# Linear attention and a two-layer FFN on one core: the fourth group's first product as seven half-size products

## The chip, the cores and the metric

The kernel runs on one core of one Trainium2 chip. The metric is the device time of one execution in microseconds (us); less is better. The core has five engines with instruction streams of their own: PE (TensorE, matrix products, with its weight loads shown as PEld), DVE (VectorE), ACT (ScalarE), POOL (GpSimd) and SP (SyncE, which here only issues DMAs). Each engine works through its own instructions in the order in which they were written, and waits at each for what it needs from the others.

## What is computed

The reference, cut to its core (B, H, S, D = 8, 8, 576, 64; the FFN's widths are 512 and 2048):

```
r = lambda x, w: np.maximum(x, 0) * w
q_p = concat(r(q, cos), r(q, sin));  k_p = concat(r(k, cos), r(k, sin))   # 128 features
kv  = einsum('bhsf,bhsd->bhfd', k_p, v);   z = sum(k_p over s)
x   = einsum('bhsf,bhfd->bhsd', q_p, kv) / (einsum('bhsf,bhf->bhs', q_p, z) + 1e-6)
h   = x @ w_in                      # (4608, 512) @ (512, 2048)
out = maximum(0.01 * h, h) @ w_out  # (4608, 2048) @ (2048, 512)
```

cos and sin depend on the position in the sequence alone.

## The kernel before

The 4608 tokens are worked in nine groups of 512 tokens: groups 0 to 7 are the first 512 tokens of batches 0 to 7, and group 8 gathers the last 64 tokens of every batch. "The fourth group" is group 3. For each batch and group these steps follow each other:

- loads of q, k and v (SP, L121 and L135), each into a staging buffer; k of batches 1 and 3 lies in the buffer `wext`.
- k's feature map, `k_token` (L253 on DVE and POOL, L251 on ACT): 9 pieces with cosine and 9 with sine, "kp" below; there is **one** kp buffer, so the pieces of batch b+1 can be written only when the kv sum of batch b is done. `v_pairs` casts v into the buffer vm (also one).
- `kv_sum` (L326): 72 small matmuls in a row, the "kv sum"; ACT copies the result out (L333).
- `q_prep`: q's feature map, four pieces of two instructions (cosine, sine), in two buffers of two pieces ("pairs"); each pair is transposed by a DMA (L363).
- `num` (L400): four times eight small matmuls, and DVE's division (L411, L415, L416) into xs; a DMA transposes xs into xT (L377).
- the first product of the FFN, x times w_in, with the leaky ReLU that gives g.
- the second product, g times w_out, and the stores of the output.

The two FFN products are done in two ways. The plain way (`ffn1`, L474): 16 units of four matmuls of 512 columns, every second one followed by one activation of 1024 columns on ACT (L482). The other way splits both factors in halves and multiplies seven times instead of eight (Winograd's form of Strassen's algorithm): seven half-size products and a number of sums. In the second product (`ffn2s`, L733) this is used from group 1 on. The sums of the weights are made once (`weight_sum`), the sums of g by DVE for each group (`g_sum`, all L526).

In the first product (`ffn1s`, L626) it is used from group F7 = 4 on. A group has four parts u; in each, seven products of four matmuls of 256 columns, and on the way seven evictions of 512 columns on ACT and two sums on DVE (`ffn1e`): b, s and u copy PSUM (L640, L642, L644), y and z add (DVE, L526), a, c, e and d are the leaky ReLU (L652). A part uses three of four PSUM banks, which rotate. It needs the sums W of w_in, made once (`w1_sum`: numbers 1, 2 and 4 go into `wext`, number 3 is made in place in w_in and so waits for the last plain first product), and four sums X of xT for each group (`x_sum`).

What sets the order is written out by hand in two layers. PE's work after the beginning is a list of *units*, each with a position: group g's second product and group g+1's first product share the positions 16g to 16g+16. All other work is a list of *steps*, each with a position out of the table TUNE; `weave` issues, ahead of every unit, the steps whose position has been reached. TUNE gives for each batch b: "kc", "ks" the places of the 18 kp pieces, "q", "v", "n" (num), "mm" (kv sum), "qT" and "x" (transposes), "L" (loads), and "e", a string that says which engine does what: four letters for q, nine for kc, nine for ks, two for v (P POOL, D DVE, A ACT). "S", "S4s", "W", "X", "T" place the sums, "We" and "Xe" their engines. Where the first product is split, the string "O" gives the order of a part: digits are products, F is half a unit of the second product, letters are evictions. "ahead" tells how many units of the second product stand before the first product of the next group begins (for groups 1 and 2).

Of the kernel before, what the change touches and what calls it, by code (L numbers as in the profile page):

```python
# [16 lines left out]
T = 9  # L17
# [3 lines left out]
def kernel(  # L21
# [15 lines left out]
    B, H, S, D = q.shape  # L37
# [12 lines left out]
    NG = B + 1  # L50
    NE = D + 2
    G7 = 1
    F7 = 4

    ctx.enter_context(tc.manual_schedule())

# [31 lines left out]
    def need(*keys):  # L88
        for key in keys:
            assert key in done, key  # L90
# [154 lines left out]
    kv = [const.tile([P, H, NE], dt.float16, name=f"kv{b}") for b in range(B)]  # L245
# [319 lines left out]
        )  # L565

    def w1_sum(bp, n, eng):
        need(("kv", 3), *(("W", bp, i) for i in {1: (), 2: (1,), 4: (2,), 3: (1,)}[n]))
        if n == 3:
            need(("f1", F7 - 1))  # L570
        done.add(("W", bp, n))
        a11, a12, a21, a22 = (w1_quarter(bp, r, d) for r in range(2) for d in range(2))
        o1, o2, o4 = (SW[i][:, bp] for i in (1, 2, 4))
        if n == 1:
            tt_op(o1, a21, a22, ALU.add, eng)
        elif n == 2:
            tt_op(o2, o1, a11, ALU.subtract, eng)
        elif n == 3:
            tt_op(a21, a11, a21, ALU.subtract, eng)
        else:  # L580
            tt_op(o4, a12, o2, ALU.subtract, eng)

    def x_sum(g, n, eng):
        need(("xT", g), *(("X", g, i) for i in {1: (), 2: (1,), 4: (2,), 3: (1,)}[n]))
        if g > F7 and n in (2, 4):
            need(("f1", g - 1))
# [213 lines left out]
    held = []  # L800
# [24 lines left out]
    for hg in range(2):  # L825
        for j in range(J):
            e = ACT if j == 3 else POOL if hg == 1 and j == 2 else DVE
# [81 lines left out]
    def f2h(g, i):  # L909
        return lambda: ffn2s(g, i // 2, (i % 2,))  # L910
# [37 lines left out]
    order = [(tt, part) for part in range(3) for tt in range(J)]  # L948
# [45 lines left out]
    for m in range(6, NFT):  # L994
        units.append((8 + m / 2, f1(1, m)))

    TUNE = {'B': {2: {'L': None,
               'e': 'PDPDDDPPDADDDPPDAAAADADD',
               'kc': [9.77, 8.81, 11.63, 10.39, 5.8, 11.57, 6.05, 9.36, 10.09],
               'ks': [9.53, 8.49, 7.12, 10.33, 12.5, 12.31, 11.64, 10.89, 9.62],  # L1000
               'mm': 13.64,
               'n': [14.2, 15.14, 16.53, 17.13],
               'q': [8.35, 8.73, 8.87, 10.0],
               'qT': [10.83, 11.12],
               'v': [8.01, 10.09],
               'x': 17.37},
           3: {'L': [2.08, 11.11, 12.82, 15.77],
               'e': 'AAAPAPADDADPAAAAAADAPADS',
               'kc': [20.89, 22.22, 20.65, 20.01, 23.27, 23.44, 20.62, 21.9, 18.49],
               'ks': [15.15, 17.93, 17.14, 16.06, 17.76, 21.94, 20.89, 19.82, 24.95],  # L1010
               'mm': 26.16,
               'n': [26.78, 28.23, 28.78, 29.48],
               'q': [15.64, 18.8, 13.77, 18.62],
               'qT': [18.98, 19.88],
               'v': [21.71, 21.6],
               'x': 30.73},
           4: {'L': [16.71, 21.32, 20.14, 20.14],
               'e': 'PADDDAADAADDAAAADDDDDDDP',
               'kc': [30.62, 29.57, 31.25, 31.74, 33.43, 33.08, 32.79, 33.57, 35.66],
               'ks': [32.92, 32.9, 30.68, 36.1, 37.07, 36.25, 36.42, 34.07, 32.95],  # L1020
               'mm': 38.04,
               'n': [39.1, 41.29, 42.88, 43.81],
               'q': [32.62, 34.78, 35.82, 36.19],
               'qT': [35.22, 37.11],
               'v': [32.65, 35.2],
               'x': 44.12},
           5: {'L': [34.11, 29.18, 40.16, 40.16],
               'e': 'ADADAAAPAAADPDADAAAPDDAP',
               'kc': [38.44, 38.15, 38.92, 39.32, 40.87, 41.72, 40.0, 43.78, 40.87],
               'ks': [38.93, 38.71, 39.75, 41.84, 41.1, 38.82, 43.11, 39.83, 43.81],  # L1030
               'mm': 47.03,
               'n': [47.67, 52.31, 51.34, 53.28],
               'q': [39.37, 39.97, 39.48, 43.05],
               'qT': [43.05, 44.13],
               'v': [43.91, 42.87],
               'x': 54.54},
           6: {'L': [42.28, 44.22, 45.5, 45.5],
               'e': 'ADAAPPPPDPDPADPADPDPAPPP',
               'kc': [53.18, 53.74, 53.6, 52.91, 53.27, 55.16, 55.42, 56.13, 58.02],
               'ks': [52.77, 51.75, 53.37, 52.12, 55.91, 60.22, 57.04, 53.88, 59.03],  # L1040
               'mm': 61.88,
               'n': [65.52, 67.68, 69.17, 71.27],
               'q': [53.1, 56.98, 57.05, 58.94],
               'qT': [58.17, 60.13],
               'v': [58.06, 56.62],
               'x': 71.75},
           7: {'L': [56.13, 58.67, 61.31, 61.31],
               'e': 'ADADDPAPADDDAAPPDAAAADPP',
               'kc': [66.43, 65.11, 67.46, 69.35, 71.81, 72.94, 73.77, 75.44, 76.57],
               'ks': [66.11, 68.9, 68.79, 69.21, 69.83, 69.79, 72.94, 73.3, 73.64],  # L1050
               'mm': 77.65,
               'n': [79.76, 83.09, 85.27, 87.09],
               'q': [68.45, 70.19, 73.41, 73.73],
               'qT': [74.58, 77.29],
               'v': [70.0, 75.7],
               'x': 91.06},
           8: {'L': [80.3, 80.97, 83.67, 84.3],
               'e': 'PDAD',
               'kc': [],
               'ks': [],  # L1060
               'mm': 1.77,
               'n': [96.19, 98.15, 99.61, 101.69],
               'q': [86.42, 87.09, 90.14, 91.17],
               'qT': [90.6, 94.58],
               'v': [],
               'x': 103.69}},
     'O': ['1b5sFF6uFF2a7yF3zcFFe4d', '1b5sFF6uF2a7yF3zcFe4dFF'],
     'S': {1: [12.21, 12.8, 18.14, 13.88, 15.3, 17.98],
           2: [26.26, 26.46, 33.47, 28.81, 29.6, 33.81],
           3: [44.93, 46.66, 45.74, 46.54, 46.47, 48.84],  # L1070
           4: [60.19, 61.22, 64.88, 60.45, 61.59, 65.79, 65.07],
           5: [75.6, 76.13, 80.5, 77.09, 78.7, 83.16, 81.99],
           6: [91.23, 91.98, 96.48, 92.12, 94.25, 96.16, 97.15],
           7: [107.64, 109.18, 113.66, 109.45, 110.7, 111.07, 111.38],
           8: [123.3, 125.17, 130.52, 123.94, 125.59, 128.31, 129.84]},
     'S4': 25.16,
     'S4s': {2: [41.14, 41.26],
             3: [56.09, 55.22],
             4: [71.56, 71.4],
             5: [88.97, 89.77],  # L1080
             6: [104.5, 104.51],
             7: [119.89, 120.83]},
     'T': [8.99, 12.77, 9.59, 14.6],
     'W': [[31.24, 32.96, 34.8, 47.53], [37.35, 38.58, 38.89, 48.2]],
     'We': ['PPDD', 'PDDP'],
     'X': {4: [47.03, 47.24, 49.45, 47.13],
           5: [61.4, 63.54, 63.57, 62.66],
           6: [77.84, 79.15, 79.25, 78.62],
           7: [94.22, 95.69, 96.01, 95.7],
           8: [109.08, 112.39, 113.4, 111.16]},  # L1090
     'Xe': {4: 'DPPD', 5: 'PDPD', 6: 'PPPP', 7: 'DDPP', 8: 'PPDD'},
     'ahead': [12, 7],
     'held': 9.31}

    for g in range(1, NG):
        last = 14
        ahead = {1: TUNE["ahead"][0], 2: TUNE["ahead"][1], NG - 1: last}.get(g, 0)
        order = [f2(g, i) for i in range(ahead)]
        left = last - ahead
        if F7 <= g + 1 < NG:  # L1100
            n = i = 0
            for u in range(4):
                for c in TUNE["O"][u == 3]:
                    if c == "F":
                        order.append((n, f2h(g, 2 * ahead + i)))
                        i += 1
                    elif c.isdigit():
                        order.append((n, f1p(g + 1, u, int(c))))
                    else:
                        order.append((n - 1 + E_AT[c], f1e(g + 1, u, c)))  # L1110
                    n += c == "F" or c.isdigit()
            assert i == 28, i
            units += [(16 * g + 16 * p / n, u) for p, u in order]
            continue
        elif g + 1 < NG:
            behind = [-(-16 * (k + 1) // left) - 1 for k in range(left)]
            for i in range(16):
                order.append(f1(g + 1, i))
                order += [f2(g, ahead + k) for k in range(left) if behind[k] == i]
        for n, u in enumerate(order):  # L1120
            units.append((16 * g + 16 * n / len(order), u))
# [30 lines left out]
    for b, t in TUNE["B"].items():  # L1152
        e = [engines[c] for c in t["e"]]
# [57 lines left out]
```

## Time and profile before

| | us |
|---|---|
| median of 3 runs | 276.87 |
| the runs | 278.65, 276.87, 276.69 |
| profiled execution, its own time | 276.07 |
| of it, span from the first to the last instruction | 274.3 |
| DVE, ACT, POOL busy in the span | 196.2, 180.4, 101.1 |

Positions and times go together as follows: position 16 (group 1's second product) begins 68.7 us after the span's start, position 32 at about 97.5, the kv sums of batches 2, 3, 4 and 5 stand at 61.3, 85.7, 107.9 and 125.1. In the rows of the profile, a line such as `L253 POOL TENSOR_SCALAR kp<-kst,cos_t 128x256 f16<-128x256 f32 x12 | 15.4, 1292 | 15.9 <-PE ...` gives line, engine, operation, output and inputs, sizes and count; then busy us and the mean ns of one; then the engine's idle time before them and what ended it. A row of a timeline gives start, length, and what; `x72` is 72 instructions in a row. L253 and L526 are lines of helpers, so the tile names tell what a row is: kp is k's map, qp q's, vm the cast v, wext and w the sums W, X and xT the sums X, g and ext the sums of g, y and ps_f the additions y and z.

### The profile page before, as it was taken

The page shows a single profiled execution, that of the slowest core. Times are in us where ns is not written, and L with a number is a line of the kernel's source. Part 1 is how long each engine was busy: PE and PEld are TensorE (multiplying, and loading weights), DVE is VectorE, ACT ScalarE, POOL GpSimd, SP SyncE. Part 2 cuts the span into 40 slices and gives each one's busy share as a digit, 9 for nine tenths or more (in the row PEclk, how much of TensorE's full clock was granted, in tenths as well). Part 3 has the DMA queues.
Part 4 walks back from the last instruction along what each step waited for, and adds up shares of the span by engine and source line. Part 5 has one row for each costly group of instructions (what it writes and reads, how often), then busy time and mean ns, then how long its engine had stood idle before and what let it go on. Part 6 is the DMA issues. An engine that isn't in the chain of part 4 may idle for free.

```text
span 274.3 us, 6865 instructions
## 1 busy us (share of the span) xinstructions
PE 265.5 (97%) x2813; PEld 212.0 (77%) x2813; DVE 196.2 (72%) x401; ACT 180.4 (66%) x310; POOL 101.1 (37%) x84
## 2 busy tenths in 40 slices
PE   7899999999999999999999999999999999999994
PEld 2575464655976586677999999999998899999983
DVE  4850597799863678786988789986798658646752
ACT  7857447497825556974898599866775567676500
POOL 2576002998509600323899290515003003000000
PEclk9999999999999999999999999999999999999999
DMA  7999999999999879999979974936475052111124
GB/s 240 358 395 410 382 400 372 376 227 291 301 179 299 322 176 238 260 229 176 377 160 256 263 235 104 196 89 146 103 165 126 4 117 76 41 38 41 60 58 115
DMA packets 77119, 57.59 MB, mean 210 GB/s; under 512 B 49312, under 2 KB 65696, under 8 KB 76704
## 3 DMA queue, kind: packets, MB, share of 16 engines
q1 hardware_dynamic: 76480, 56.63, 73.0%
q10 hardware_dynamic: 608, 0.52, 0.6%
q8 instruction: 22, 0.36, 0.6%
q14 instruction: 9, 0.07, 0.1%
HBM read 36.70 MB, written 9.44 MB: 168 GB/s over the span
## 4 chain that ended last, share of the span: by engine, by line
PE 71%; DMA 18%; POOL 4%; DVE 3%; SPq 2%; issue 2%; ACT 0%; POOLq 0%; DVEq 0%
PE ps L733 33%; PE ps_f L626 22%; DMA qst<-in_q_dram 10%; PE ps_h L474 10%; DMA wext<-in_moe_w_in_dram 4%; DMA qpT<-qp 3%; PE ps_num L400 3%; PE ps_kv L326 2%; POOL qp L253 2%; POOL kp L253 2%; PE ps_f L733 1%; SPq L135 1%; SPq L167 1%; DVE xs L416 1%; DVE ext L526 0%
## 5 line engine op out<-in xcount | busy, mean ns | idle before, releaser
L733 PEld LDWEIGHTS <-g 128*128 128x128 f16 x640 | 61.7, 98 | 8.2 <-ACT g L482 0.6
L733 PE MATMUL ps<-w,g 128*128 128x256 f16 x496 | 64.8, 273 | 0.4 <-ACT g L482 0.4
L474 PE MATMUL ps_h<-xT,w 128*128 128x512 f16 (+1 forms) x272 | 59.3, 367 | 0.1
L482 ACT ACTIVATE g<-ps_h 128x1024 f16<-128x1024 f32 x32 | 32.2, 1023 | 23.9 <-PE ps_h L474 23.9
L474 PEld LDWEIGHTS <-w 128*128 128x128 f16 x272 | 29.6, 114 | 20.6
L652 ACT ACTIVATE g<-ps_f 128x512 f16<-128x512 f32 x60 | 34.7, 596 | 8.5 <-PE ps_f L626 6.1
L626 PEld LDWEIGHTS <-w 128*128 128x128 f16 x320 | 34.6, 114 | 0.8
L626 PE MATMUL ps_f<-xT,w 128*128 128x256 f16 x240 | 33.3, 273 | 0.0
L733 PE MATMUL ps<-T,ext 128*128 128x256 f16 x240 | 32.1, 273 | 0.0
L733 PEld LDWEIGHTS <-ext 128*128 128x128 f16 x256 | 24.8, 98 | 3.1 <-issue 0.2
L626 PEld LDWEIGHTS <-wext 128*128 128x128 f16 x240 | 26.4, 113 | 0.8 <-issue 0.2
L253 POOL TENSOR_SCALAR kp<-kst,cos_t 128x256 f16<-128x256 f32 (+1 forms) x15 | 18.2, 1225 | 18.7 <-PE ps_kv L326 15.9
L526 DVE TENSOR_TENSOR ext<-g 128x512 f16<-128x512 f16 (+1 forms) x23 | 14.6, 640 | 12.1 <-ACT g L482 10.0
L526 DVE TENSOR_TENSOR y<-ps_f,s 128x512 f32<-128x512 f32 x20 | 13.8, 689 | 11.0 <-PE ps_f L626 9.1
L526 DVE TENSOR_TENSOR ext<-ps,ext 128x512 f32<-128x512 f32 x16 | 11.0, 690 | 12.8 <-PE ps L733 11.7
L416 DVE TENSOR_TENSOR xs<-ps_num,rden 128x512 f16<-128x512 f32 x28 | 19.4, 691 | 1.0
L626 PE MATMUL ps_f<-X,wext 128*128 128x256 f16 x128 | 19.2, 272 | 0.0
L652 ACT ACTIVATE g<-y 128x512 f16<-128x512 f32 x20 | 12.6, 630 | 9.2 <-DVE y L526 9.2
L644 ACT COPY u<-ps_f 128x512 f32<-128x512 f32 x20 | 11.7, 587 | 10.2 <-PE ps_f L626 10.1
L526 DVE TENSOR_TENSOR osb<-ps,ext 128x512 f32<-128x512 f32 x23 | 15.8, 685 | 3.7 <-PE ps L733 3.7
L526 POOL TENSOR_TENSOR X<-xT,X 128x512 f16<-128x512 f16 x7 | 8.8, 1262 | 22.9 <-PE ps_f L626 16.1
L733 PE MATMUL ps<-ext,g 128*128 128x256 f16 x128 | 17.1, 272 | 0.0
(116 smaller groups left out, 444.5 us busy)
## 6 DMA issues: line engine op xcount, KB each, us to landing
out_dram<-osb SPq DMA_DIRECT2D x32, 256.0 KB, 3.2
qst<-in_q_dram SPq DMA_DIRECT2D x7, 1024.0 KB, 8.0
kst<-in_k_dram SPq DMA_DIRECT2D x5, 1152.0 KB, 9.0
vst<-in_v_dram SPq DMA_DIRECT2D x5, 1152.0 KB, 7.5
w2st<-in_moe_w_out_dram SPq DMA_DIRECT2D x3, 1024.0 KB, 12.8
vst<-in_v_dram SPq DMA_DIRECT2D x4, 576.0 KB, 6.6
ext<-in_moe_w_in_dram SPq DMA_DIRECT2D x4, 512.0 KB, 10.7
kst<-in_k_dram SPq DMA_DIRECT2D x2, 576.0 KB, 7.5
```

The lines of the kernel that those rows point to most:

```text
L135: nc.sync.dma_start(st[nm, b][:, sl].rearrange("p c j d -> p c (j d)"), rows[:, sl])
L253: eng.tensor_scalar(out=o, in0=i, scalar1=0.0, scalar2=col, op0=ALU.max, op1=ALU.mult)
L326: nc.tensor.matmul(ps[:, o, (c - lo) * NE : (c - lo + 1) * NE], lhsT=st["kp", b][sl, c, j, :], rhs=vm[sl, c, j, :], start=(j == 0), stop=( ...
L400: nc.tensor.matmul(ps[lo:hi, h // 4, (h % 4) * NE : (h % 4 + 1) * NE], lhsT=qpT[:, h, lo:hi], rhs=kv[b][:, h, :],)
L416: nc.vector.tensor_tensor(out=xs, in0=ps[:, :, 0 : 4 * NE].rearrange("p a (b e) -> p a b e", e=NE)[:, :, :, 0:D], in1=rden.rearrange("p (a ...
L474: nc.tensor.matmul(ps[:, m % 2, lo:hi], lhsT=w1[m // 4, c][0][:, w1[m // 4, c][1], m % 4 : 512 : 4], rhs=xT[:, lo // P : hi // P, c, :], s ...
L482: nc.scalar.activation(st["g", g][:, m - 1 : m + 1, :], ps, AF.Lrelu)
L526: eng.tensor_tensor(out=o, in0=a, in1=b, op=op)
L626: nc.tensor.matmul(ps[:, mi * HT : (mi + 1) * HT], lhsT=a[:, c, 2 * r0 + mi : 512 : 4], rhs=b[:, c], start=(n in (1, 5) and mi == 0 and c ...
L644: nc.scalar.copy(u1, B_)
L652: nc.scalar.activation(st["g", g][:, m : m + 2, r * HT : (r + 1) * HT], {"a": A, "c": y22, "e": E, "d": B_}[e].rearrange("p (m t) -> p m t ...
L733: nc.tensor.matmul(ps[:, tt], lhsT=a[:, i, tt * P : (tt + 1) * P], rhs=b[:, i], start=(first and i == 0), stop=(i == NPR - 1 and (apart or ...
```

## The change

Group 3's first product is done as seven half-size products too (F7 = 3), so its 16 plain units and 8 activations leave, and 28 products with 28 evictions on ACT and 8 sums on DVE come. It needs four sums X for group 3. The W sums are placed earlier (their position moves from 31.24 to 24.80 for the first, from 48.2 to 35.67 for the last), and `w1_sum` asks for the kp pieces of batch 3 instead of its kv sum. In group 2's second product 8 units (16 halves) stand ahead instead of 7, and the 12 halves that are left lie in the parts of group 3's first product by four new strings of "O". The places and engines of most steps of batches 2 to 5 are set anew, those of 6 to 8 slightly.

```
-    F7 = 4
+    F7 = 3
...
     def w1_sum(bp, n, eng):
-        need(("kv", 3), *(("W", bp, i) for i in {1: (), 2: (1,), 4: (2,), 3: (1,)}[n]))
+        need(*(("kp", 3, j, f, 0) for j in range(T) for f in (0, D)), *(("W", bp, i) for i in {1: (), 2: (1,), 4: (2,), 3: (1,)}[n]))
...
     TUNE = {'B': {2: {'L': None,
-               'e': 'PDPDDDPPDADDDPPDAAAADADD',
+               'e': 'PDPDDDPPDADDPPPAPAAADDDD',
...
-               'q': [8.35, 8.73, 8.87, 10.0],
+               'q': [7.49, 7.91, 9.16, 10.33],
...
            3:
-               'e': 'AAAPAPADDADPAAAAAADAPADS',
+               'e': 'APAPPPAPDDAPAAAAAPAADAAA',
...
            4:
-               'e': 'PADDDAADAADDAAAADDDDDDDP',
+               'e': 'AADADAPAADPDAPDDDDPDDDDP',
...
            5:
-               'e': 'ADADAAAPAAADPDADAAAPDDAP',
+               'e': 'APAPPDPPPDPDDDDADPAPDDAP',
-               'kc': [38.44, 38.15, 38.92, 39.32, 40.87, 41.72, 40.0, 43.78, 40.87],
-               'ks': [38.93, 38.71, 39.75, 41.84, 41.1, 38.82, 43.11, 39.83, 43.81],
-               'mm': 47.03,
+               'kc': [39.02, 39.31, 41.53, 41.24, 40.23, 42.8, 42.37, 44.86, 42.56],
+               'ks': [40.41, 39.97, 41.78, 45.51, 44.13, 41.98, 45.77, 42.39, 46.09],
+               'mm': 47.0,
...
-     'O': ['1b5sFF6uFF2a7yF3zcFFe4d', '1b5sFF6uF2a7yF3zcFe4dFF'],
+     'O': ['1b5sF6u2aF7y3zcF4ed', '1b5sF6u2aF7y3zcF4ed', '1b5sF6u2aF7y3zcF4ed', '1b5sF6u2aF7y3zc4edF',
+           '1b5sFF6uFF2a7yF3zcFFe4d', '1b5sFF6uF2a7yF3zcFe4dFF'],
...
-     'W': [[31.24, 32.96, 34.8, 47.53], [37.35, 38.58, 38.89, 48.2]],
-     'We': ['PPDD', 'PDDP'],
-     'X': {4: [47.03, 47.24, 49.45, 47.13],
+     'W': [[24.8, 25.9, 27.1, 32.85], [29.07, 30.81, 32.09, 35.67]],
+     'We': ['PDPD', 'PPPD'],
+     'X': {3: [34.5, 35.23, 35.51, 37.21],
+           4: [46.97, 48.08, 49.48, 48.2],
...
-     'ahead': [12, 7],
-     'held': 9.31}
+     'ahead': [12, 8],
+     'held': 5.78}
...
         if F7 <= g + 1 < NG:
-            n = i = 0
+            order = [(i, f2h(g, i)) for i in range(2 * ahead)]
+            n = i = 2 * ahead
             for u in range(4):
-                for c in TUNE["O"][u == 3]:
+                for c in TUNE["O"][u if ahead else 4 + (u == 3)]:
                     if c == "F":
-                        order.append((n, f2h(g, 2 * ahead + i)))
+                        order.append((n, f2h(g, i)))
                         i += 1
```

POOL's order up to kv sum 2 was q, kp, q, kp, kp, kp (a q is one piece of two instructions) and becomes q, kp, kp, kp, q, kp, kp, kp. Between kv sums 4 and 5 POOL had kp, kp, v, kp and gets kp, q, kp, kp, kp, q, kp, v, kp, kp.

## The prediction

> **What bounds the kernel now.** I read the page first (busy time, slices), then the chain of waits, then the timelines of PE and POOL around the instructions that the change moves.
>
> ```profile
> span 274.3 us, 6865 instructions
> PE 265.5 (97%) x2813; PEld 212.0 (77%) x2813; DVE 196.2 (72%) x401; ACT 180.4 (66%) x310; POOL 101.1 (37%) x84
> ```
>
> PE is busy for 97% of the span, at a granted clock of 0.9 or more in all 40 slices. A matmul taken away is worth its whole pace, and every new wait of PE costs its whole length. The pace is read from the chain of waits:
>
> ```profile
> 107.93 1.25 PE ps_kv L326 x72
> ...
> 115.02 1.73 PE ps_h L474 x8
> 116.75 0.87 PE ps L733 x8
> ...
> 125.06 1.25 PE ps_kv L326 x72
> ```
>
> A 512-column matmul takes 1.73/8 = 0.216 us, a 256-column one 0.87/8 = 0.109 us. The two x72 rows are the kv sums of batches 4 and 5. Each reads all 18 kp pieces of its batch; there is one kp buffer, so no piece of batch 5 can be written before kv sum 4 has ended, and PE can't start kv sum 5 before the last piece is there. So the bracket from kv sum to kv sum (1) has a PE length and (2) must hold all kp work of one batch on each engine. Busy time by bracket (us; PE, PEld, DVE, ACT, POOL, each with its count):
>
> ```profile
> 86.91:107.93 21.02, 20.56 (x166) 14.08 (x166) 15.71 (x40) 11.31 (x18) 6.52 (x4) 1.00 0.88 265
> ...
> 109.18:125.06 15.88, 15.88 (x125) 10.25 (x126) 11.42 (x28) 12.87 (x21) 4.69 (x4) 1.00 0.94 240
> ...
> 126.31:150.16 23.85, 23.85 (x240) 21.94 (x242) 21.52 (x41) 19.41 (x36) 21.09 (x16) 1.00 0.99 246
> ```
>
> The second row is the bracket that the change fills most: POOL does only 4.69 us in 15.88. In the third POOL has 21.09 of 23.85 and PE still has no idle time.
>
> The third thing to see is that kv sum 2 has no slack today. POOL, then PE:
>
> ```profile
> 46.86 2.00 POOL L253 TENSOR_SCALAR qp<-qst,cos_t 128x512 f16<-128x512 f32 x1 [2.23 <-PE ps_o L500]
> 48.85 2.00 POOL L253 TENSOR_SCALAR qp<-qst,sin_t 128x512 f16<-128x512 f32 x1
> 50.82 1.14 POOL L253 TENSOR_SCALAR kp<-kst,sin_t 128x256 f16<-128x256 f32 x1
> 51.94 2.50 POOL L253 TENSOR_SCALAR qp<-qst,cos_t 128x512 f16<-128x512 f32 x1
> 54.42 2.15 POOL L253 TENSOR_SCALAR qp<-qst,sin_t 128x512 f16<-128x512 f32 x1
> 56.55 1.57 POOL L253 TENSOR_SCALAR kp<-kst,sin_t 128x256 f16<-128x256 f32 x1
> 58.11 3.24 POOL L253 TENSOR_SCALAR kp<-kst,cos_t 128x256 f16<-128x256 f32 x2
> ```
>
> ```profile
> 61.30 1.35 PE L326 MATMUL ps_kv<-vm,kp 64*128 64x66 f16 x72
> ...
> 68.07 0.28 PE L733 MATMUL ps<-w,g 128*128 128x256 f16 x1 [0.35 <-ACT g L482]
> 68.47 0.43 PE L400 MATMUL ps_num<-kv,qpT 128*128 128x66 f16 x8
> ```
>
> POOL's last kp piece ends at 58.11 + 3.24 = 61.35, and PE starts the sum at 61.30. Whatever is added to POOL before it, PE waits for.
>
> **The change part by part.** Prices on POOL come from the groups by shape:
>
> ```profile
> L253 POOL TENSOR_SCALAR kp<-kst,cos_t 128x256 f16<-128x256 f32 x12 | 15.4, 1292 | 15.9 <-PE ps_kv L326 15.9
> L253 POOL TENSOR_SCALAR kp<-kst,sin_t 128x256 f16<-128x256 f32 x9 | 11.9, 1328 | 1.1 <-DMA kst<-in_k_dram 1.1
> L253 POOL TENSOR_SCALAR qp<-qst,cos_t 128x512 f16<-128x512 f32 x4 | 9.0, 2255 | 2.2 <-PE ps_o L500 2.2
> L253 POOL TENSOR_SCALAR qp<-qst,sin_t 128x512 f16<-128x512 f32 x4 | 8.6, 2161 | 0.0
> L261 POOL CAST vm<-vst 128x1152 f16<-128x1152 f32 x6 | 7.0, 1176 | 4.3 <-DMA vst<-in_v_dram 4.3
> ```
>
> *PE's own work.* 16 units of 4 matmuls of 512 columns go (64 x 0.216 = 13.8), 28 products of 4 matmuls of 256 come (112 x 0.109 = 12.2): -1.6 us. The 28 halves of group 2's second product stay 28; one unit more of them stands ahead, which counts nothing. Weight loads: 112 for 64, but PEld has 21.94 of 23.85 in a bracket of such halves and PE is full there: nothing.
>
> *kv sum 2.* POOL's queue up to it was q, kp, q, kp x3; it becomes q, kp x3, q, kp x3: two pieces more. The first q waits for the same q load and starts at 46.86 as before. From 50.82: kp 1.14, two kp at about 1.36 (between 1.14 and 1.57), q 4.65, three kp at 1.6 (as 3.24/2), ends 64.1. PE waits 64.1 - 61.3 = 2.8. Ends: all at the fastest rows (1.14, 2.00) POOL is done at 46.86 + 8.0 + 6.8 = 61.7, +0.4; with all six at 1.6, +3.4. I take 2.8, since the neighbouring rows ran at that rate. What comes back: the q transpose of pair 1 (landing 68.42, PE at 68.47 after 0.29 idle) is issued about 1 us earlier and PE comes later, so that wait goes, and a 0.2 wait before the num at 65.66 (it waits for DVE's division) too: -0.5. The 0.35 for ACT's g stays; its cause is PE's own last unit. Net +2.3.
>
> *kv sum 2 to 4.* POOL gets four W sums (2.12 each) and the X sums 1 and 2 between kv sums 3 and 4, with 4 kp and a v: about 17.4 us where PE needs 19.3. What ends last there is xT of group 3, which landed at 99.58, 12.7 after kv sum 3's end: X1, X2 (1.26 each) and one kp behind it end at 16.5. Cover 2.8: costed at nothing. W sums that wait for each other across POOL and DVE hold DVE up for some 2.6 us where it idled 5.37 us before (86.76): nothing.
>
> *kv sum 4 to 5.* PE's nominal length: 31 products and halves x 0.437 = 13.55, four num x 0.26, together 14.6. POOL's queue in it: cos kp x5 (6.5), sin kp x2 (2.7), two q of two instructions (8.8), one v (1.2): 19.1 where it was 4.69. It starts 0.17 after kv sum 4 (109.35 against 109.18 before), and the piece that comes last is read 0.2 after the sum's start, so kv sum 5 starts at 19.1, not 14.6: +4.5. Ends: all at the fastest rows (1.14, 2.00, 1.15) 17.1, +2.5; all at rows slowed most (1.6, 2.5, 1.32) 22.5, +7.9. I take the means, because most of this batch's pieces lie beside DVE work of the mixed kind that made those means.
>
> *Evictions.* Eight L482 activations (1023 ns) become 28 of 0.59 us on ACT and eight additions of 0.69 on DVE. ACT has in this bracket 21 of them (12.4), two q (2.9), two kp (1.0), v 1.15 and kv 0.6: 18.0 by the row means, some 15.1 when starts overlap by the 0.1 us that the timeline shows: more than 14.6. Product 6 waits for copy b behind e and d, product 4 for y only one half (0.44) and product 3 after product 7. Following the order with these rows I find waits of PE of 0.1, 0.6, 0.4, 0.75, 0.25 and 0.5: 2.6 us, but they end before POOL's last piece: hidden under the 4.5. If POOL were in time, they would be what is left.
>
> *SP.* The q transposes of group 5 wait for POOL's q, and the loads of q, k, v 6 and x's transpose of group 4 stand behind them. Transpose 1 goes out about 14.2 after kv sum 4, k 6 at some 17 (17.9 before): no later against kv sum 5. Nothing.
>
> *Later groups.* Between kv sums 5 and 6 PE's length is 26.3 with 21.7 on POOL; between 6 and 7 22.4 with 8.8. ACT stays near 80%. PE's instructions cover this; at most 1 us if some step misses (the longest such wait before was 0.25, at 210.65).
>
> **Sum.** -1.6 + 2.3 + 4.5 = +5.2. On the profiled execution (276.07, of it 274.3 span) that is 281.3; its time lies 0.80 under the median of the runs (276.87), so the forecast for the median is 282.1.
>
> **A rule beside the rows.** POOL's kp took 1.14 at 135.69 (5.63 for five) while DVE mostly read PSUM, and 1.69 at 141.30 beside DVE's g<-g,ext with two inputs from SBUF. The Trainium skill, GPSIMD Engine Reference, section 1 "Specifications", says that POOL shares its SBUF interface with VectorE and contends with instructions of two SBUF inputs or of a 2-port mode; by that rule, the trace agrees, and the sum would come out as in rival 1 instead of at 282.1.
>
> **Rivals.**
> 1. *POOL slowed further by DVE.* The bracket holds six of DVE's g additions with two SBUF inputs; at 1.69 - 1.14 = 0.55 for each, the 17.1 of undisturbed POOL becomes 20.4 and the time 283.4; at the slowed rows throughout 22.5, 285.5. For: DVE has 16 us of work in the 14.6. Against: at 134 to 141 DVE was nearly full and POOL ran at 1.14.
> 2. *The eviction loop is the bound.* If the waits behind ACT and DVE come to twice my 2.6, they pass POOL's 4.5 by 0.7: 282.8; three times, 285.4. For: ACT is over its share. Against: between 126 and 150 ACT had 19.41 of 23.85 without a wait of PE.
> 3. *Not slower: POOL at its undisturbed rate.* With 1.14 and 2.00, kv sum 2 costs 0.4 - 0.5 and kv sum 5 2.5 (or the loop's 2.6): -1.6 - 0.1 + 2.5 = +0.8, 277.7. It decides once the two waits of PE together fall under 4.9 us, about a mean kp of 1.2. For: 1.14 is the commonest row. Against: around 56 to 61 none ran so.
> 4. *The count alone*, no new wait: 275.3. It needs POOL 19 us of work in 14.6.
>
> **Chances.** Forecast 0.62 (280.6 to 283.6: kv sum 2 net 1.8 to 2.9, kv sum 5 3.5 to 5.5); rival 1 0.13, rival 2 0.08, rival 3 0.12, rival 4 0.05. The range leaves out rival 4, the lower half of rival 3 and the top of rival 1: 278.8 to 285.2. One per cent (2.77 us) is about what a measurement of this kernel tells from no change. Faster by over that 0.02 (the best of rival 4), within it 0.14 (rivals 3 and 4), slower 0.84.
>
> **What would show it.** PE idle before L326 with releaser POOL kp, some 2.8 us near 61 and some 4.5 us near 130; POOL without a gap between kv sums 4 and 5; L626 672 times at 0.109 apart. Wrong if PE has no idle time there, if its long waits stand at L626 for ACT or DVE, or if POOL's kp take 1.14 throughout.

## The result and the profile after

The changed kernel takes 286.78 us (median of four runs, 286.14 to 287.8), the kernel before 276.97 (four runs, 276.69 to 278.65). The ratio is 1.0345 (95% interval 1.0289 to 1.04): 9.8 us slower, where 5.2 had been forecast (282.1, with a range of 278.8 to 285.2). A run more than 1.5% above the fastest of its kernel, as one run each of four experiments below is, is left out of the medians and ratios. The profiled execution took 287.37 us, 285.6 of it span; its granted clock has a mean of 0.985, against 0.999 before.

The page of the changed kernel, its first lines and the rows of PE and of the granted clock in 40 slices of 7.1 us:

```profile
span 285.6 us, 7009 instructions
PE 267.8 (94%) x2861; PEld 218.4 (76%) x2861; DVE 204.3 (72%) x407; ACT 185.3 (65%) x320; POOL 130.9 (46%) x103
...
PE   6999999956999899898999999999999999999994
...
PEclk9999999995999999999999999999999999999998
```

Two things are to be seen. In the ninth slice (57 to 64 us) PE is busy for half of the time, and in the tenth (64 to 71) the granted clock is 0.5. And PE's busy time has grown by 2.3 us although 1.6 us of work were taken away: in the rows below, four matmuls of 512 columns take 1.90 us at a clock of 0.50, as long as eight take at 1.00.

So I measured PE not by busy time but by what it takes over its pace: the distances between starts of matmuls, less the median distance of that form in the kernel before, summed by stretch of time (us; waits and lost clock are both in it):

| stretch | before | after | "two pieces back" (below) |
|---|---|---|---|
| 0 to 45 | 5.21 | 4.88 | 5.31 |
| 45 to 60 | 0.54 | 0.54 | 0.57 |
| 60 to 80 (kv sum 2) | 1.19 | 8.66 | 0.94 |
| 80 to 105 (kv sum 3) | 0.89 | 1.68 | 2.25 |
| 105 to 145 (kv sums 4, 5) | 0.69 | 4.88 | 4.67 |
| 145 to 200 | 0.29 | 0.75 | 1.34 |
| 200 to the end | 1.32 | 1.73 | 1.72 |

The column after has 13.0 more than the column before; less the 1.6 us of work that went, 11.4, beside a difference of the two spans of 11.3. So the whole loss of the profiled execution is in the table, and 7.5 of it stands at kv sum 2. The timeline of PE there, after (start, duration, engine, line, operation, tile; in brackets the idle time before it and its releaser):

```profile
60.96 0.23 PE L326 MATMUL ps_kv<-vm,kp 64*128 64x66 f16 x4
66.41 2.05 PE L326 MATMUL ps_kv<-vm,kp 64*128 64x66 f16 x68 [5.22 <-POOL kp L253]
68.40 1.90 PE L474 MATMUL ps_h<-xT,w 128*128 128x512 f16 x4
70.09 0.65 PE L400 MATMUL ps_num<-kv,qpT 128*128 128x66 f16 x8
```

The releaser is the one that was named; the wait is 5.22 of idle time (5.39 by the distance of the starts, which is what I give for waits at kv sum 2 from here on) instead of 2.8. And the rows behind it are slow: 68 matmuls of the sum in 2.05 (72 took 1.35 before), four matmuls of 512 columns in 1.90 (eight took 1.89). Busy time by window, after (bounds; sum; then PE, PEld, DVE, ACT, POOL with counts; granted clock; DMA share; GB/s):

```profile
54.00:61.00 7.00, 7.00 (x36) 3.55 (x35) 7.00 (x12) 6.67 (x10) 7.00 (x4) 1.00 1.14 236
61.10:66.40 5.30, 0.09 (x4) 0.00 (x0) 2.62 (x4) 0.99 (x1) 5.26 (x4) 0.91 1.15 302
66.40:72.20 5.80, 5.79 (x84) 3.54 (x85) 1.36 (x4) 1.83 (x3) 3.48 (x3) 0.50 0.99 336
72.20:79.00 6.80, 6.45 (x68) 4.93 (x67) 4.94 (x13) 6.11 (x11) 6.80 (x4) 1.00 0.12 39
```

The second row is the wait: POOL works 5.26 of 5.30, PE does nothing. In the third PE works without a gap at a clock of 0.50; by the records of the clock it fell 4.2 us into the wait, at 65.40, and stayed there for 6.83 us, to 72.23. Of these PE worked 5.8, and at half clock that is half lost: 2.9 us. So the 7.5 is a wait of 5.4, a clock of 2.9 and 0.8 back from shorter waits.

Why POOL was late, its timeline after:

```profile
47.55 2.00 POOL L253 TENSOR_SCALAR qp<-qst,cos_t 128x512 f16<-128x512 f32 x1 [2.24 <-DMA qst<-in_q_dram]
49.54 2.00 POOL L253 TENSOR_SCALAR qp<-qst,sin_t 128x512 f16<-128x512 f32 x1
51.51 4.84 POOL L253 TENSOR_SCALAR kp<-kst,sin_t 128x256 f16<-128x256 f32 x3
56.34 2.15 POOL L253 TENSOR_SCALAR qp<-qst,cos_t 128x512 f16<-128x512 f32 x1
58.48 3.07 POOL L253 TENSOR_SCALAR qp<-qst,sin_t 128x512 f16<-128x512 f32 x1
61.53 4.83 POOL L253 TENSOR_SCALAR kp<-kst,cos_t 128x256 f16<-128x256 f32 x3
```

The queue is the forecast one, q, kp x3, q, kp x3, but it ends at 66.36 instead of 64.1. The 2.26 us are: the q load 0.69 later (47.55 for 46.86), the second q 5.22 for 4.65 (+0.57), the six kp 9.67 for 8.66 (+1.0). The six pieces took 1.14, 1.82, 1.91 and 2.58, 1.14, 1.14. DVE beside them, after:

```profile
58.56 1.21 DVE L526 TENSOR_TENSOR w<-w 128x2048 f16<-128x2048 f16 x1
59.69 1.16 DVE L261 CAST vm<-vst 128x1152 f16<-128x1152 f32 x1
60.77 0.68 DVE L526 TENSOR_TENSOR ext<-g 128x1024 f16<-128x1024 f16 x1
61.37 1.21 DVE L526 TENSOR_TENSOR T<-w,T 128x2048 f16<-128x2048 f16 x1
62.51 0.68 DVE L526 TENSOR_TENSOR ext<-ext,g 128x1024 f16<-128x1024 f16 x1
63.11 0.61 DVE L526 TENSOR_TENSOR ext<-g 128x512 f16<-128x512 f16 x1
70.77 0.17 DVE L411 TENSOR_SCALAR den<-ps_num 128x8 f32<-128x8 f32 x1 [7.05 <-PE ps_num L400]
```

The sums of L526 read two inputs from SBUF. POOL's piece beside the three that start at 61.37, 62.51 and 63.11 took 2.58; from 63.7 on DVE was idle, and the two pieces there took 1.14 each. The q half beside the rows at 58.56, 59.69 and 60.77, two sums and the cast of v between them, took 3.07 where 2.00 is the shortest. The cast reads one input, and it counts as well: DVE's cast of v also runs at 53.47, beside the piece of 1.82 (with 0.3 us of a sum), and in "sums behind the num" below a piece that has the cast and no sum beside it takes 1.83. The piece of 1.91 has a sum beside it (54.14, 1.21 us).

### The profile page after: what moved, and what is told of

It is laid out like the page before. It is cut to its first block, busy times and chain, and to the rows that moved or that the text cites. A ratio compares the mean times of both kernels' runs of the same rounds, so it can differ in the third digit from the quotient of the medians.

```text
span 285.6 us, 7009 instructions
## 1 busy us (share of the span) xinstructions
PE 267.8 (94%) x2861; PEld 218.4 (76%) x2861; DVE 204.3 (72%) x407; ACT 185.3 (65%) x320; POOL 130.9 (46%) x103
## 4 chain that ended last, share of the span: by engine, by line
PE 60%; DVE 7%; POOL 6%; issue 1%; ACT 1%; POOLq 0%; DVEq 0%
PE ps L733 28%; PE ps_f L626 21%; PE ps_h L474 6%; DVE ext L526 4%; POOL qp L253 3%; POOL kp L253 3%; PE ps_kv L326 2%; PE ps_num L400 2%; PE ps_f L733 1%; DVE osb L526 1%; DVE xs L416 1%; ACT g L482 1%; DVE y L526 0%; POOL vm L261 0%; DVE kp L253 0%
## 5 line engine op out<-in xcount | busy, mean ns | idle before, releaser
L652 ACT ACTIVATE g<-ps_f 128x512 f16<-128x512 f32 x72 | 41.3, 596 | 8.1 <-PE ps_f L626 5.5
L474 PE MATMUL ps_h<-xT,w 128*128 128x512 f16 (+1 forms) x208 | 45.7, 372 | 0.1
L626 PE MATMUL ps_f<-xT,w 128*128 128x256 f16 x288 | 40.3, 273 | 0.0
L482 ACT ACTIVATE g<-ps_h 128x1024 f16<-128x1024 f32 x24 | 24.2, 1024 | 21.2 <-PE ps_h L474 21.2
L626 PEld LDWEIGHTS <-wext 128*128 128x128 f16 x288 | 31.4, 114 | 2.2 <-issue 1.4
L253 POOL TENSOR_SCALAR kp<-kst,cos_t 128x256 f16<-128x256 f32 (+1 forms) x22 | 27.1, 1243 | 8.1 <-PE ps_kv L326 4.5
L526 DVE TENSOR_TENSOR y<-ps_f,s 128x512 f32<-128x512 f32 x24 | 16.5, 688 | 13.4 <-PE ps_f L626 9.6
L652 ACT ACTIVATE g<-y 128x512 f16<-128x512 f32 x24 | 15.1, 630 | 11.1 <-DVE y L526 11.1
L526 DVE TENSOR_TENSOR ext<-g 128x512 f16<-128x512 f16 (+1 forms) x24 | 16.7, 707 | 6.7 <-ACT g L482 4.4
L526 DVE TENSOR_TENSOR ext<-ps,ext 128x512 f32<-128x512 f32 x16 | 11.0, 687 | 11.3 <-PE ps L733 9.9
L526 DVE TENSOR_TENSOR osb<-ps,ext 128x512 f32<-128x512 f32 x23 | 15.8, 685 | 4.3 <-PE ps L733 4.1
L526 DVE TENSOR_TENSOR ps_f<-ps_f,u 128x512 f32<-128x512 f32 x24 | 16.7, 696 | 1.8 <-PE ps_f L626 0.3
L326 PE MATMUL ps_kv<-vm,kp 64*128 64x66 f16 x576 | 12.1, 196 | 6.2 <-POOL kp L253 5.9
```

Of the source, the lines that this page charges most:

```text
L253: eng.tensor_scalar(out=o, in0=i, scalar1=0.0, scalar2=col, op0=ALU.max, op1=ALU.mult)
L326: nc.tensor.matmul(ps[:, o, (c - lo) * NE : (c - lo + 1) * NE], lhsT=st["kp", b][sl, c, j, :], rhs=vm[sl, c, j, :], start=(j == 0), stop=( ...
L474: nc.tensor.matmul(ps[:, m % 2, lo:hi], lhsT=w1[m // 4, c][0][:, w1[m // 4, c][1], m % 4 : 512 : 4], rhs=xT[:, lo // P : hi // P, c, :], s ...
L482: nc.scalar.activation(st["g", g][:, m - 1 : m + 1, :], ps, AF.Lrelu)
L526: eng.tensor_tensor(out=o, in0=a, in1=b, op=op)
L626: nc.tensor.matmul(ps[:, mi * HT : (mi + 1) * HT], lhsT=a[:, c, 2 * r0 + mi : 512 : 4], rhs=b[:, c], start=(n in (1, 5) and mi == 0 and c ...
```

## The experiments

The theory after this comparison: the excess over the forecast is (a) POOL's pieces stretched by DVE's sums (the cast was not tried apart), and (b) the clock that falls when PE waits long; in group 3's first product the waits are POOL's, as forecast. The rivals: the excess is in the eviction loop or in the later groups; the lost clock is no effect of the wait.

**Two pieces back.** The change undone in one place: two kp pieces of batch 2 go from POOL to the engines that had them (batch 2's row of engines).

```
- 'e': 'PDPDDDPPDADDPPPAPAAADDDD',
+ 'e': 'PDPDDDPPDADDDPPAAAAADDDD',
```

> The changed kernel with POOL's two extra kp pieces of batch 2 given to ACT (sine 3) and DVE (cosine 8); all else as changed. Theory A (kv sum 2 waits for POOL, 5.4 us, and the long wait halves the granted clock for 6.8 us, some 2.9 us more): both go, since POOL is done some 2 x 1.9 us earlier and at most 1.5 us of wait is left; 286.8 - 7 = 279 to 280.5, granted clock 1.0 throughout. Theory B (the split product of group 3 costs most, kv sum 2 little beyond its wait): 286.8 - 3 = 283.5 or more.

Measured: 281.05 us (281.23 over all four; ratio 1.0143, 1.0116 to 1.017; the kernel before on the same chip 276.83). PE, "two pieces back":

```profile
61.42 1.32 PE L326 MATMUL ps_kv<-vm,kp 64*128 64x66 f16 x72
```

In this profile there is no wait and the clock is 1.0 throughout; one run took 286.49 at a clock of 0.993 and has no profile, so what it waited for is not shown. The two pieces cost 286.78 - 281.05 = 5.7 us between the medians. What is left over the kernel before, 5.0 between the profiled spans, is -1.6 and 6.7 more in the third column of the table than in the first, of which 1.4 stand at 80 to 105 and 4.0 at 105 to 145.

**Two pieces alone.** The other way round: the kernel before, with the two pieces given to POOL and nothing else.

```
- 'e': 'PDPDDDPPDADDDPPDAAAADADD',
+ 'e': 'PDPDDDPPDADDPPPDPAAADADD',
```

> The kernel before with only the two pieces (sine 3, cosine 8 of batch 2) moved to POOL; their places stay as before. Theory A: POOL ends some 3 to 4 us later, PE waits that long ahead of kv sum 2; 277.0 + 3 to 4 = 280 to 281, or 283 if the wait is long enough to halve the clock. Theory B: under 279.

Measured: 282.27 (ratio 1.0184, 1.0128 to 1.024; before 276.83): +5.4, about what undoing them in the changed kernel gave. PE, and a window behind the wait, "two pieces alone":

```profile
61.44 0.23 PE L326 MATMUL ps_kv<-vm,kp 64*128 64x66 f16 x4
65.31 2.05 PE L326 MATMUL ps_kv<-vm,kp 64*128 64x66 f16 x68 [3.63 <-POOL kp L253]
```

```profile
65.30:68.70 3.40, 3.39 (x72) 2.48 (x73) 0.00 (x0) 1.30 (x3) 3.40 (x2) 0.50 1.07 257
```

A wait of 3.81 and 3.41 us at half clock. Of its four runs the one with a clock of 1.0 took 279.72, those with 0.985 to 0.994 took 282.21 to 283.66: so the runs part by the clock, by some 2.5 to 4 us, the length of their waits being known for the profiled one alone.

**Kept busy.** To part the clock from the wait: the changed kernel, with 20 matmuls into an unused tile ahead of kv sum 2, so that PE works while it waits.

```
+ if b == 2:
+     warm_ps = psum("o", [P, MAIN], dt.float32, "ps_idle")
+     for _ in range(20):
+         nc.tensor.matmul(warm_ps, lhsT=ident, rhs=w2[:, 0, :])
```

> The changed kernel with 20 matmuls of 512 columns (20 x 0.216 = 4.3 us) that write an unused PSUM tile, put ahead of kv sum 2; they do no part of the computation. Theory A: the wait for POOL stays where it is in time, PE fills it, the granted clock stays at 1.0 and the 2.9 us of half-speed work go: about 284. If the halved clock were no cost of its own: 286.8 as now. If the wait were not POOL's: 291.

Measured: 284.34 (ratio 1.0277, 1.0251 to 1.0302). PE, then a window, "kept busy":

```profile
61.36 4.48 PE L324 MATMUL ps_idle<-w,ident 128*128 128x512 f16 x20
65.77 1.32 PE L330 MATMUL ps_kv<-vm,kp 64*128 64x66 f16 x72
...
68.17 1.89 PE L478 MATMUL ps_h<-xT,w 128*128 128x512 f16 x8
```

```profile
66.40:72.20 5.80, 5.55 (x83) 3.46 (x75) 3.49 (x8) 4.62 (x8) 4.85 (x3) 1.00 0.99 356
```

PE works through the wait, and the kernel is 2.4 us faster than the changed one: matmuls that nobody reads save time, since the clock stays at 1.00 (0.998 to 1.0 in its four runs, 0.985 to 0.993 in those of the changed kernel). That is (b), and it rules out that the clock fell for another reason. Of the 5.7 us, some 2.4 are the clock and 284.34 - 281.05 = 3.3 the wait that stays. The split is rough: in this profile PE is at the sum at 61.36 and POOL's last piece ends at 65.76, so the wait that is filled is 4.4, not 5.4.

What makes the clock fall, and come back, can be read from all 13 profiles together. Within a profile its changes lie whole multiples of 3.413 us apart: after, it rose at 3.96, fell at 65.40 (18 x 3.413 later) and rose at 72.23 (2 x 3.413). So I cut each profile into windows of 3.413 us on that grid and took PE's busy time in each. Of the windows at full clock within the spans, the 13 with 1.39 us or less were each followed by half clock, and none with 1.58 or more was. Of those at half clock, the two with 1.74 and 2.40 were followed by another, the six with 3.12 or more by full clock. Seven of the 13 falls are at the very end, where PE's work is over; the other six:

| profile | wait of PE, by starts | busy in the window ahead of the fall | half clock for |
|---|---|---|---|
| after | 5.39 | 0.00 | 6.83 |
| "sums later" | 4.85 | 0.57 | 3.41 |
| "all mended" | 4.60 | 0.66 | 6.83 |
| "two pieces alone" | 3.81 | 0.00 | 3.41 |
| "sums behind the num" | 3.35 | 0.28 | 3.41 |
| "four ahead" | 2.33 | 1.25 | 3.41 |

A wait of 3.39 in "last two to DVE" lay across two windows with 1.72 and 1.90 of work, and the clock stayed. So the length of a wait alone does not decide, but how much of it falls into one window; and the stretch at half clock is two windows long where the wait reaches far into the first of them (1.0 us after, 1.7 in "all mended", at most 0.3 in the others). Where the grid lies differs from execution to execution (the clock first rose between 3.85 and 7.13 us after the span's start). The Trainium skill, TensorE: Matmul & The Clock Gate, "Part 1: The HAM clock gate (the "warmup" mystery)", gives a free-running window of 3413 ns of which one idle one halves the clock. The grid agrees; that the window must be idle does not, by the 1.25 us of work in the one of "four ahead".

**Sums later.** To test (a): the weight sums that DVE makes beside POOL's pieces are set behind kv sum 2 in the order of the work.

```
- 'T': [9.7, 12.91, 10.62, 14.85],
+ 'T': [13.7, 13.9, 13.8, 14.85],
```

> The changed kernel with DVE's three sums of w_out (1.2, 1.6 and 1.2 us, two inputs from SBUF) moved from before kv sum 2 to behind it; POOL's own work is untouched. If DVE's sums are what stretches POOL's pieces there (1.8 to 2.6 us where 1.14 is the shortest): POOL ends near 62.7, the wait falls from 5.4 to some 1.7 us, the clock stays at 1.0: 286.8 - 3.7 - 2.9 = 280.2. If POOL's length is its own: 286.8, or more if the sums come late behind kv sum 2.

Measured: 285.41 (ratio 1.0306, 1.0281 to 1.0331) where 280.2 was expected, and inconclusive. DVE does not wait for kv sum 2, so the sums only slid to 60.35 to 64.03, beside POOL's last three pieces; these took 2.36, 2.48 and 1.13, the last one when DVE was idle. The wait was 4.85.

**Sums behind the num.** The same with places behind DVE's first division, for which DVE has to wait.

```
- 'T': [9.7, 12.91, 10.62, 14.85],
+ 'T': [14.3, 14.6, 14.5, 14.86],
```

> The changed kernel with DVE's sums of w_out behind the division of num 0 of group 2, which waits for kv sum 2, so that DVE can't run them while POOL makes its last pieces (in the experiment before, they only slid to 60 to 64, beside those pieces). Contention theory: the pieces take 1.1 to 1.6 instead of 1.9 to 2.6, POOL ends 2 to 3 us earlier, the wait is 2 to 3 us instead of 5.4 and the clock stays at 1.0: 286.8 - 5 = 281.5 to 283, less what the late sums cost behind kv sum 2 (up to 1). If POOL's pieces take as long without them: 286.8 or more.

Measured: 286.39 (ratio 1.0371, 1.0322 to 1.0421). POOL, "sums behind the num":

```profile
47.45 1.99 POOL L253 TENSOR_SCALAR qp<-qst,cos_t 128x512 f16<-128x512 f32 x1 [2.29 <-PE ps_o L500]
...
51.41 4.08 POOL L253 TENSOR_SCALAR kp<-kst,sin_t 128x256 f16<-128x256 f32 x3
55.47 2.11 POOL L253 TENSOR_SCALAR qp<-qst,cos_t 128x512 f16<-128x512 f32 x1
57.56 2.25 POOL L253 TENSOR_SCALAR qp<-qst,sin_t 128x512 f16<-128x512 f32 x1
59.79 3.90 POOL L253 TENSOR_SCALAR kp<-kst,cos_t 128x256 f16<-128x256 f32 x3
...
68.64 4.07 POOL L253 TENSOR_SCALAR qp<-qst,cos_t 128x512 f16<-128x512 f32 x1 [1.89 <-DMA qpT<-qp]
```

The same ten instructions that took 18.8 us after (47.55 to 66.36) take 16.2 (47.45 to 63.69): (a) is shown. PE's wait at kv sum 2 falls from 5.4 to 1.7; of these 3.7, 2.7 are POOL's earlier end, and 1.0 is that PE reaches the sum later in this execution (61.97 for 60.96). The sums took their cost along. At 67.33 to 72.48 DVE makes them in a row, and POOL's q half beside them takes 4.07 instead of 1.99; the division behind them comes late, and PE, "sums behind the num":

```profile
63.75 1.25 PE L326 MATMUL ps_kv<-vm,kp 64*128 64x66 f16 x68 [1.54 <-POOL kp L253]
...
73.67 0.60 PE L400 MATMUL ps_num<-kv,qpT 128*128 128x66 f16 x8 [3.17 <-DVE xs L416]
```

That wait halves the clock at 73.37 for 3.41 us. The gain at the one place is lost at the other.

**Last two to DVE.** For the wait at kv sum 5: POOL's last two pieces of batch 5 go to DVE.

```
- 'e': 'APAPPDPPPDPDDDDADPAPDDAP',
+ 'e': 'APAPPDPPPDPDDDDADDADDDAP',
```

> The changed kernel with the two last kp pieces on POOL between kv sums 4 and 5 (sine 4 and 6 of batch 5) given to DVE. If POOL's length is what sets kv sum 5 (the forecast's step, 4.5 us): POOL ends 2.7 us earlier and some 2.5 us are won, 284.3. If the waits behind ACT and DVE use up most of that bracket first: only the 0.9 us wait at kv sum 5 itself goes, 286.

PE after (between kv sums 4 and 5, the rows with a wait of 0.3 or more, and the two rows of kv sum 5):

```profile
121.14 0.60 PE L626 MATMUL ps_f<-X,wext 128*128 128x256 f16 x4 [0.73 <-ACT ps_f L640]
...
125.04 0.41 PE L400 MATMUL ps_num<-kv,qpT 128*128 128x66 f16 x8 [0.41 <-DVE xs L416]
...
132.22 0.60 PE L626 MATMUL ps_f<-X,wext 128*128 128x256 f16 x4 [0.31 <-ACT ps_f L640]
...
134.08 0.36 PE L326 MATMUL ps_kv<-vm,kp 64*128 64x66 f16 x12
135.16 1.13 PE L326 MATMUL ps_kv<-vm,kp 64*128 64x66 f16 x60 [0.71 <-POOL kp L253]
```

and "last two to DVE":

```profile
118.29 0.60 PE L626 MATMUL ps_f<-X,wext 128*128 128x256 f16 x4 [0.91 <-ACT ps_f L640]
...
122.19 0.42 PE L400 MATMUL ps_num<-kv,qpT 128*128 128x66 f16 x8 [0.41 <-DVE xs L416]
...
129.89 0.60 PE L626 MATMUL ps_f<-X,wext 128*128 128x256 f16 x4 [0.83 <-ACT ps_f L640]
...
131.75 1.32 PE L326 MATMUL ps_kv<-vm,kp 64*128 64x66 f16 x72
```

Measured: 286.11 (ratio 1.0347, 1.0327 to 1.0367; after 1.0345), no gain. The profiled execution is the fastest of its five runs, 284.70, and the only one with a clock of 1.0, so I compare this stretch alone. POOL's wait at kv sum 5 is gone, and the waits for ACT's copy in the loop have grown by 0.7. From kv sum 4's start to kv sum 5's end it is 20.80 us after (115.49 to 136.29) and 20.60 here (112.47 to 133.07). So POOL is not alone in setting this stretch: the loop, which waits here for ACT's copies, is as long as POOL's queue, within a few tenths.

**Five attempts to mend the rest.** All keep the two pieces back.

*Num places back*: the four nums of batch 3 at their places of before.

```
- 'n': [27.1, 27.32, 28.52, 29.41],
+ 'n': [26.78, 28.23, 28.78, 29.48],
```

> The first experiment (two pieces back) with the four num of group 3 at the places that they had before (26.78, 28.23, 28.78, 29.48 instead of 27.1, 27.32, 28.52, 29.41). If the waits for the division between two num (0.55 and 0.62 where the kernel before has one of 0.61) come from the places: 281.2 - 0.6 = 280.6. If not: 281.2.

281.18 (ratio 1.0147, 1.0126 to 1.0168) against 281.05: no gain. The waits moved (1.5 for DVE's division from 91.1 on, 1.3 for a sum of DVE from 103.9 on). What held the division up were two sums of g, 2.25 and 1.58 us beside POOL's W sums.

*Four ahead*: four units (eight halves) instead of eight of group 2's second product ahead of group 3's first, the other four spread over its parts, and the X sums of group 3 earlier.

```
- 'O': ['1b5sF6u2aF7y3zcF4ed', ...
+ 'O': ['1b5sF6uF2aF7yF3zcFe4d', ...
- 'X': {3: [34.5, 35.23, 35.51, 37.21],
+ 'X': {3: [33.3, 34.0, 34.2, 35.0],
- 'ahead': [12, 8],
+ 'ahead': [12, 4],
```

> The first experiment with 4 units of the second product ahead instead of 8, so that each part of group 3's first product has five halves between its products instead of three, and the X sums of group 3 placed earlier. If the waits between kv sums 4 and 5 come from products that follow too closely on the evictions that they need: most of the 2 us of waits at L626 go, 279.5; POOL's length (18.3 us) may then set kv sum 5 and leave 280.5. If ACT and DVE simply have too much to do: no better than 281.2. A late xT of group 3 would show as a wait near 100 and cost 1 us or more.

284.86 (ratio 1.0306, 1.026 to 1.0351): 3.8 worse. The product now starts before its X sums are made (0.73 and 1.34 for POOL at 104 to 107), the waits in the loop are not shorter, and the longest halves the clock for 3.41 us at 123:

```profile
122.52 0.60 PE L626 MATMUL ps_f<-X,wext 128*128 128x256 f16 x4 [2.17 <-ACT ps_f L640]
```

*Less POOL, later q*: POOL's last two pieces of batch 5 on DVE as above, and the first q of batch 5 later, so that ACT's eviction does not stand behind it.

```
- 'q': [38.63, 39.54, 40.8, 41.67],
+ 'q': [39.9, 39.95, 40.8, 41.67],
```

> The first experiment with the two last kp pieces of batch 5 given from POOL to DVE and the first q of batch 5 (1.3 us on ACT) behind the copies b and s of the second part instead of ahead of them. If that q is what makes product 6 wait for copy b (0.96 us at 113.5) and POOL what makes kv sum 5 wait (0.89): 281.2 - 1.7 = 279.5. If the waits only move on to the next product: 280.5 to 281.2.

280.69 (ratio 1.0147, 1.0111 to 1.0183) against 281.05: nothing. The waits move from one product to the next (0.74 behind ACT at 115.9, 0.83 at 126.2).

*W on DVE*: the W sums that the change gave to POOL, all on DVE.

```
- 'We': ['PDPD', 'PPPD'],
+ 'We': ['DDDD', 'DDDD'],
```

> The first experiment with all eight W sums on DVE (0.7 us each where POOL takes 2.1 to 2.7). If POOL's W sums and DVE slow each other between kv sums 3 and 4 (a sum of g of 0.69 took 2.25 at 86.9): the waits for the division (1.2 us in two) shrink and those between 80 and 105 fall from 2.3 to about 1: 281.2 - 1.2 = 280. If DVE's own load is the cause: 281.2 or worse.

279.77 (ratio 1.0111, 1.0094 to 1.0128; before 276.65), 1.3 less than with the two pieces back alone, and the best of all variants; it does not reach the kernel before. DVE's sums did become shorter, as expected. After, with POOL at W sums of 2.12 to 2.45 us:

```profile
93.90 1.94 DVE L526 TENSOR_TENSOR ext<-g 128x1024 f16<-128x1024 f16 x1 [2.90 <-ACT g L482]
...
96.79 1.57 DVE L526 TENSOR_TENSOR ext<-ext,g 128x1024 f16<-128x1024 f16 x1
```

and "W on DVE":

```profile
87.01 0.69 DVE L526 TENSOR_TENSOR ext<-g 128x1024 f16<-128x1024 f16 x1 [3.47 <-ACT g L482]
87.61 0.69 DVE L526 TENSOR_TENSOR wext<-w,wext 128x1024 f16<-128x1024 f16 x1
```

A sum of g that takes 0.69 takes 1.94 beside POOL's; and a W sum that takes POOL 2.12 takes DVE 0.69. So POOL's sums and DVE's stretch each other, and PE waits for the division behind the sums of g.

But that is not where the 1.3 came from. Between 80 and 105, PE loses 2.70 us here and 2.25 with the two pieces back, where a fall to about 1 had been expected: the waits for the division there went from 0.38 and 0.46 to one of 0.36, and a wait of 1.73 for another sum of DVE stands ahead of 104.6. The profiles differ in favour of "W on DVE" behind 105 alone, 5.8 against 7.7, and there "num places back", with POOL's W sums as they were, has 5.9. The time that was expected, 280, came out by luck; why this variant is the best stays open.

*All mended*: num places back, less POOL with the later q, and W on DVE together.

> All mends together: the two pieces of batch 2 back, W sums on DVE, the num places of before, the last two pieces of batch 5 on DVE, the first q of batch 5 later. What is left of waits against the kernel before should be those behind ACT and DVE in group 3's first product, some 2.5 us, less the 1.6 us won: 278 to 279.5. It would have to lose 2 us less than that to beat the kernel before (277.0), which I don't expect. If the waits come from elsewhere: 281.

281.92 (ratio 1.019, 1.0167 to 1.0213): worse than "W on DVE" alone by 2.2, and not the 278 to 279.5 that was expected. Edits that each gave little or nothing do not add up to that; each moves the queues of two engines. Its profiled execution, of 287.86 us, shows how thin the cover at kv sum 2 is, even with the two pieces back:

```profile
59.63 6.15 POOL L253 TENSOR_SCALAR kp<-kst,cos_t 128x256 f16<-128x256 f32 x2
```

POOL's first q stood at 47.67 here, 0.68 later than with the two pieces back, and the last two pieces 1.67 later, at 59.63. So they came to lie beside DVE's sums and cast at 59.11 to 63.66: the first took 5.03, the second, with DVE idle, 1.13. In "two pieces back" the same two took 2.44 together. PE, at the sum from 61.19 on, went on with it at 65.84: in this execution 1.7 us of lateness on POOL became a wait of 4.6 and 6.83 us at half clock.

## Why the prediction was wrong, step by step

- *The direction* was right, and the places: POOL's kp at kv sums 2 and 5. *PE's own work*, -1.6, fits the balance of the table.
- *kv sum 2, net +2.3*: this is the step that failed. It came to 7.5 in the profile, and the two pieces to 5.7 between medians. That POOL's last piece would be waited for was right; two terms were off. First, the wait itself, 2.8 forecast and 5.4 measured. POOL's end was 66.36, not 64.1, since I priced the pieces by the rows beside them (1.36 and 1.6) and not by what DVE does beside them: 1.91 and 2.58 beside its sums of two SBUF tensors, 1.82 beside its cast of v, 1.14 when it is idle. "Sums behind the num" showed it, 16.2 us for 18.8. The upper end that I gave, +3.4 for all six at 1.6, comes to +3.7 by its own rows, and was no bound. Another 0.69 is a q load that landed later; "the same q load ... starts at 46.86 as before" was not so. The profiles give no sign that this is an effect of the change: over all 13 this q starts at 46.86 to 47.67, in "two pieces alone", which has the loads of before, at 47.45. PE's earlier arrival, 60.96 for 61.30, gave the last 0.3. Second, a term was missing: PE's waits were costed at their own length, and the clock behind them at nothing, though a wait can halve it. That is some 2.4 us by "kept busy" and 2.9 by the windows.
- *A rule beside the rows*: I weighed POOL against DVE's two-input sums as rival 1 for the stretch between kv sums 4 and 5 alone. The Trainium skill, GPSIMD Engine Reference, section 1 "Specifications", names just such instructions of VectorE as the ones that contend with POOL; the traces agree (1.14 against 2.58 for one form of piece), and it struck at kv sum 2, to which I had not applied it.
- *kv sum 2 to 4: nothing*. It cost 0.8 by the table, and 1.3 counted from the start of kv sum 3 to that of kv sum 4 (2.2 over the pace, 0.9 before). I checked POOL's length against PE's (that cover held) and gave DVE's sums their durations of before, 0.69; beside POOL's W sums they take up to 1.94, and PE waited 0.77 and 0.46 for the divisions behind them, where before there was one such wait, of 0.45.
- *kv sum 4 to 5: +4.5*. The table has 4.2 more for the stretch from 105 to 145; from the start of kv sum 4 to the end of kv sum 5 it is 20.80 against 14.6 of nominal length and 2.5 for the two sums, so 3.7. The size was about right and the account of it half right: POOL's last piece ended 18.3 us after kv sum 4 (forecast 19.1), but the waits ahead of kv sum 5 that I found by the rows (2.6 in sum) came to some 2.7, of which 0.4 was for a division, and POOL's last piece left only 0.9 of wait. "Last two to DVE" took these 0.9 away and won 0.2 of the stretch. So POOL and rival 2, the eviction loop, bound it about equally. That the loop's waits would end before POOL's held; that they cost nothing, since POOL alone decides, did not. That the sum of the two came near the forecast is in part luck.
- *Later groups, at most 1*: +0.9 by the table (145 us to the end).
- Open: which of ACT and DVE is the tighter one in the loop of group 3 (two variants moved its waits without shortening them); how much of POOL's stretching at kv sum 2 is the cast's and how much the sums'; and where the gain of "W on DVE" comes from.

## What to carry to other kernels

When work is moved to POOL, price it by what DVE will be doing beside it at that moment, not by the mean of its form, and price DVE's work beside it anew as well. When PE is nearly full, a forecast of a wait of some 2 us or more needs a second term, with a chance, for the clock behind it: here waits of 2.33 to 5.39 us halved it, one of 3.39 did not, and which one does depends on how it falls on a grid that the kernel does not set. Where the wait can't be taken away, matmuls that nobody reads can be worth their place. Where two engines' queues in a stretch are about as long as each other, taking work from one buys almost nothing: add up both before you name the bound.

## What was not expected of the hardware

- The clock fell to 0.5 for 3.41 or 6.83 us within the kernel, after single waits of PE of 2.33 ("four ahead") to 5.39 us; 20 matmuls that nobody reads (4.48 us) prevented it and made the kernel 2.4 us faster.
- Its changes lie on a grid of 3.413 us. A window with up to 1.39 us of work of PE was followed by half clock, one with 1.58 or more never; from half clock it rose behind windows with 3.12 or more, and did not behind 1.74 and 2.40. These are the bounds of 13 profiles of this kernel and its variants.
- One form of POOL instruction, 128x256 f32 to f16, took from 1.14 to 2.58 us in one profile and 5.03 in another ("all mended"), by what DVE did at the time; the 128x512 one took 1.99 to 4.07 in "sums behind the num".
- DVE suffers as well: 0.69 became 1.94 for a 128x1024 f16 sum beside POOL's sum of 128x1024 f16.
